# Queue order in the first feed-forward unit of an attention and Fourier-mixing kernel, and the steps at which v is loaded

## The chip, the core and the metric

The kernel runs on one core of a Trainium2 chip. The core has five engines, each with its own queue of instructions, which it takes in order: TensorE (PE: matmuls and transposes into PSUM), VectorE (DVE), ScalarE (ACT), GpSimd (POOL) and SyncE (SP), which here only issues DMAs. GpSimd issues DMAs too. Engines wait for each other, and for DMAs, through semaphores. A wait at the head of a queue holds back everything behind it on that engine.

The metric is the device time of one execution in microseconds (us). Three runs of the kernel before the change gave 2347.01, 2349.23 and 2350.73, so the median is 2349.23.

## What is computed

An attention block with talking heads feeds a Fourier mixing and a feed-forward block. The sizes are 8 batches, 12 heads, 448 rows, 64 columns for each head, so a model width of 768 and a feed-forward width of 3072. All is in float32.

```python
scores = scale * np.matmul(q, k.transpose(0, 1, 3, 2))
scores = np.einsum('bhij,hg->bgij', scores, w_pre)
scores = scores - np.max(scores, axis=-1, keepdims=True)
attn = np.exp(scores)
attn = attn / (np.sum(attn, axis=-1, keepdims=True) + 1e-09)
attn = np.einsum('bhij,hg->bgij', attn, w_post)
x = np.matmul(attn, v)           # then (B, H, S, D) -> (B, S, H*D)
...
X = np.fft.fft(np.fft.fft(x, axis=1), axis=2)
u = x + np.real(X)
un = (u - mean(u)) / np.sqrt(var(u) + 1e-06)
out = u + np.maximum(un @ w_ch1, 0.0) @ w_ch2
```

## The kernel before

**Attention part** (`mix_phase`). Each batch takes 23 steps, so there are 184 (`TOT`). Everything is put into lists with due times (`due(kind, at, fn)`) and emitted step by step. Within a step the operations follow a hand-written order that alternates between even and odd steps. In this part the order of emission is kept on PE, DVE, ACT and POOL, and a scheduler places SyncE's instructions. At each step the following happens:

- A gather brings rows of the scores from `Sb` into `Kr` (L605: four DMAs of 105 KB on SyncE, issued two steps before their use). TensorE mixes the heads on them (L616).
- ScalarE takes the exponential (L630), GpSimd scales by the reciprocal sums (L640), TensorE mixes again (L650), VectorE transposes (L663), and at some steps TensorE multiplies with v (L680).
- q, k and v of the next batch are loaded on GpSimd's DMA queue (L534, L543). v comes in three pairs of heads, each in two parts of 224 KB. The three buffers are single, so a part is loaded after the last use of its buffer by the batch before. `AT_V` holds the due steps: (3, 4), (5, 6) and (7, 7) of a batch.

When a batch has its attention rows `X`, GpSimd folds them for the Fourier transform. The steps of it are kept in the list `folds`: for each of two parities `pairs` twice (L745), `sides` (L750) and `quarters` (L759, L760); for the second pair of row groups come four times `both` (L766) at the end. The transform itself is two matmul stages (L789 and L805). VectorE adds the result to `X` (L816, L818), and the rows go to the scratch memory `u` or, reversed, `v` (L837 on SyncE; L828 and L834 on GpSimd). These stores wait in the list `later` and are emitted a step after their rows are done.

**Feed-forward part** (`ffn_phase`). The rows of all batches are cut into 7 tiles of 512. The hidden width is cut into 6 chunks. A unit is one chunk on one tile, `n = c * 7 + t`, and has two halves: `first` (hidden layer, L1169, with weights `w1t`) and `second` (output layer, L1247, with weights `w2t`). Both use a Strassen-like scheme with seven products.

The first unit overlaps with the end of the attention part: the last batch's Fourier steps are still to be done. What is left of them is a list `parts`, and `next_part()` puts one between two products. So in unit 0 these things happen on each queue:

- TensorE: the seven products of `first`, then the seven of `second`. Between the products of `second` stand the transposes of the next tile, `turn(1, x)` (L1108), for four groups of 128 rows, and some parts (L789, L805).
- VectorE: statistics of tile 1 (L1088, L1089), and adds from PSUM to the tile's rows (L1254).
- GpSimd: the foldings of the last batch (`fold_rest()`), and then `power(1)` (L375 to L378), which makes scale and bias from the statistics.
- ScalarE: `norm(1, x)` (L1099, scale and bias on 128 rows) and evictions of the transposes (L1110).
- SyncE: loads of the tiles' rows (`load_u`, L1067: twelve row pieces for a tile), loads of `w1t` and `w2t` (L1071, L1075: seven of 384 KB each), stores of tile 0's transposed rows to scratch (L1417: seven of 384 KB), stores of results (L1256) and of tile 1's transposed rows (L1119).

The chain to follow is stats, power, norm, turn. Transposes go to a PSUM buffer `psQ`; there are two of these, and the fourth product of `second` uses the same two.

Before the unit a small block keeps the emission order on PE, DVE and POOL for `lead.total` and `fold_rest`. The loop over units keeps it on PE and DVE alone; the scheduler places GpSimd's, SyncE's and ScalarE's instructions.

Of the kernel before, what the change touches and what calls it, by code (L numbers as in the profile page):

```python
# [60 lines left out]
TOT = B * GS  # L61
# [22 lines left out]
NTB = B * S // TB  # L84
# [3 lines left out]

AT_T = ((5, 9), (15, 17), (13, 15))
AT_L = ((-4, -3), (-2, -1), (0, 1), (2, 7), (11, 12), (13, 14))  # L90
AT_V = ((3, 4), (5, 6), (7, 7))
AT_QK = ((0, 2, 1), (0, 1, 2), (0, 1, 2), (1, 2, 2),
         (0, 1, 2), (0, 1, 2), (0, 1, 2), (0, 1, 2))
AT_AV = ((1, 2, 4), (0, 1, 3), (1, 3, 5), (1, 2, 4))
# [15 lines left out]
NC = 6  # L110
NM = DFF // 2 // P
NK = DM // 2 // P
FM = NM // NC
# [299 lines left out]
def mix_phase(ctx, tc, rest, ident, q, k, v, w_pre, w_post, u_scr, u_rev, wts, lead):  # L413
# [6 lines left out]
    nc = tc.nc  # L420
# [27 lines left out]
    pend, folds, later = [], [], []  # L448
# [60 lines left out]
    first = {}  # L509
# [333 lines left out]
    fill = {"QK": [], "AV": [], "full": [], "none": []}  # L843
# [7 lines left out]
    for b in range(B):  # L851
# [30 lines left out]
        for n in range(NG):  # L882
# [3 lines left out]
            at, gi = AT_X[n]  # L886
# [44 lines left out]
    ET = mybir.EngineType  # L931
    with tc.manual_schedule(engines={ET.PE, ET.DVE, ET.Activation, ET.Pool}):
        while s <= TOT - GS + AT_X[-1][0]:
            old = len(later)
            n = take("none", s)
# [30 lines left out]
        flush()  # L966
        wts.deal(1000)

    def fold_rest():
        while folds:  # L970
            folds.pop(0)()

    def part(fn, tile_fn):
        for _ in range(len(later)):
            later.pop(0)()
        while later and not fn:
            later.pop(0)()
        ms.append(tile_fn)
        if fn:
            for e in fn():  # L980
                e()

    assert not any(fill[k] for k in ("QK", "AV", "none"))
    return fold_rest, [lambda t, fn=fn: part(fn, t)
                       for _, _, fn in fill["full"] + [(0, 0, None)]]

# [7 lines left out]
ORDER = (0, 4, 5, 1, 6, 2, 3)  # L996
# [4 lines left out]
DEEP = 2  # L1001
# [6 lines left out]
def ffn_phase(ctx, tc, rest, ident, u_scr, u_rev, wts, ub_scr, out, fold_rest,  # L1008
# [4 lines left out]
    nc = tc.nc  # L1013

    def pool(name, bufs=1, **kw):
        return ctx.enter_context(
            tc.tile_pool(name=name, bufs=bufs, reuse_waits="tile", **kw))

    pub = pool("pub", 3)
# [4 lines left out]
    once = ExitStack()  # L1024
# [7 lines left out]
    pps = [pool("pps" + k, space=bass.MemoryType.PSUM) for k in "QPR"]  # L1032
    beside = ExitStack()
# [19 lines left out]
    us, ubs, w1, w2, wt = {}, {}, {}, {}, {}  # L1053
    right = {}
# [4 lines left out]
    def load_u(t):  # L1059
        if t % 3:  # L1060
            u = pu.tile([P, NT2, DM], F32, name="u", tag="u")
            us[t] = [u[:, x, :] for x in range(NT2)]
        else:
            us[t] = [lead.rows() for _ in range(NT2)]
        for x in range(NT2):
            for p0, m, src in _u_pieces(t, x, u_scr, u_rev):
                nc.sync.dma_start(out=us[t][x][p0:p0 + m, :], in_=src)  # L1067
# [5 lines left out]
    def load_w2(c, i):  # L1073
        w2[i] = pw2.tile([P, FM, DH], F32, name="w2t", tag=f"w2t{i}")
        nc.sync.dma_start(out=w2[i][:, :, :], in_=wts.w2[c][i])  # L1075
# [68 lines left out]
    def first(n, st, beside):  # L1144

        c, t = divmod(n, NTB)
        deep = c >= DEEP
        seed = n >= NTB + 2
        h = st["h"] = ph.tile([P, 7, FM, HT], F32, name="h", tag="h")
        if deep:  # L1150
            hq = st["hq"] = right["hq"].tile([P, 7, 4, P], F32, name="hq", tag="hq")
        h11, h22, h21, hs1, hs2, h12, h12s = (h[:, x] for x in range(7))
        norms = c == 0 and t + 1 < NTB
        vec = nc.vector
        ps = {}
        done = 0
        for k, i in enumerate(ORDER):
            if deep and t == 0:
                halves(ORDER2[k], (nc.vector, nc.gpsimd)[k % 2])
            if i in OPENS and ACC[i] not in ps:  # L1160
                ps[ACC[i]] = ps_tile(ACC[i])
            p = ps[ACC[i]].rearrange("p (m t) -> p m t", m=FM)
            ub = ubs.pop((n, i))
            for m in range(FM):
                for kc in range(NK):
                    for fn in beside.pop(done, ()):
                        fn()
                    done += 1
                    mm = nc.tensor.matmul(p[:, m, :], w1[i][:, kc, m * P:(m + 1) * P],  # L1169
                                          ub[:, kc, :],  # L1170
                                          start=i in (0, 4, 1)[:3 - seed] and m == kc == 0,
                                          stop=kc == NK - 1, skip_group_check=True)
                    if n == k == m == kc == 0:
                        tc.keep_in_program_order(mm)
            if i == 0 and seed:
                ps["Q"] = ps_tile("Q")
                nc.scalar.copy(out=ps["Q"][:, :], in_=ps["P"][:, :])
            elif i == 0:
                nc.scalar.copy(out=h11, in_=p)
            elif i == 4:  # L1180
                nc.scalar.copy(out=h22, in_=p)
            elif i == 5:
                nc.scalar.copy(out=h21, in_=p)
            elif i == 1 and seed:
                nc.scalar.activation(h11, p, ACTF.Relu)
            elif i == 1:
                vec.tensor_tensor(h11, h11, p, op=ALU.add)
                nc.scalar.activation(h11, h11, ACTF.Relu)
            elif i == 6:
                vec.tensor_tensor(h22, h22, p, op=ALU.add)  # L1190
                nc.scalar.activation(h22, h22, ACTF.Relu)  # L1191
                if deep:
                    quarters(nc.gpsimd, hq, h, H11, H22 + 1)
            elif i == 2:
                vec.tensor_tensor(h21, h21, p, op=ALU.add)
                nc.scalar.activation(h21, h21, ACTF.Relu)
            else:
                nc.scalar.activation(h12, p, ACTF.Relu)
            x = k - 2 * (n == 0)
            if norms and 0 <= x < NT2:  # L1200
                stats(t + 1, x)
                if x == NT2 - 1:
                    power(t + 1)
            if (n == 0 and k < 2) or (n == 1 and k not in (1, 2)):
                next_part()
                if n == 0 and k == 1:
                    fold_rest()
            if deep:
                wts.deal(DEALS[t > 0][k])
            elif i != 2:  # L1210
                wts.deal(2 if norms else 3 if c == 0 else 4)
            if i == 2:
                vec.tensor_tensor(hs1, h21, h22, op=ALU.add)
                vec.tensor_tensor(hs2, hs1, h11, op=ALU.subtract)
                if deep:
                    quarters(vec, hq, h, HS2, HS2 + 1)
                vec.tensor_tensor(h21, h11, h21, op=ALU.subtract)
            if t == NTB - 1 and c + 1 < NC:
                load_w1(c + 1, i)
            if NTB <= n + 1 < NC * NTB:  # L1220
                new_ub(n + 1, i)
                nc.sync.dma_start(out=ubs[n + 1, i][:, :, :],
                                  in_=ub_scr[(n + 1) % NTB][i])
        if deep:
            quarters(nc.gpsimd, hq, h, H12, H12 + 1)
            wts.deal(0)
        else:
            vec.tensor_tensor(h12s, h12, hs2, op=ALU.subtract)
        assert not beside
# [158 lines left out]

    for i in ORDER:
        load_w1(0, i)  # L1390
    load_u(1)
    us[0] = lead.u
    ET = mybir.EngineType
    with tc.manual_schedule(engines={ET.PE, ET.DVE, ET.Pool}):
        for n in range(1, 4):
            lead.total(n, pub)
        fold_rest()
    for i in ORDER:
        ubs[0, i] = lead.ub[i]
    with tc.manual_schedule(engines={ET.PE, ET.DVE}):  # L1400
        for i in ORDER:
            load_w2(0, i)
        parts_ = [(c, k) for c in range(1, NC) for k in range(NK + FM)]
        for n in range(DEEP * NTB):
            c, t = divmod(n, NTB)
            if c == 0 and 0 < t < NK + FM + 1:
                wts.add(*parts_.pop(0))
            while c and sum(o[1] for o in wts.ops) < 52:
                wts.add(*parts_.pop(0))
            wts.deal(0)  # L1410
            if n + 2 < NTB:
                load_u(n + 2)
            st = {}
            first(n, st, {})
            if n == 0:
                for i in ORDER:
                    nc.sync.dma_start(out=ub_scr[0][i], in_=lead.ub[i])  # L1417
            second(n, st)
            if c == 0:
                wts.deal(1000)  # L1420
            if n == 1:
                assert not parts
                rest.close()
                beside.close()
                pps.append(pool("ppy", space=bass.MemoryType.PSUM))
            if n == NTB - 1:
                once.close()
                for name, bufs in (("wt", 1), ("hq", 1), ("od", 9)):
                    right[name] = pool("p" + name, bufs, side="right")

    wts.eng = nc.sync
    SEAM = {49: 0, 50: 1, 51: 1, 52: 1, 53: 2, 54: 2, 55: 3, 56: 3, 57: 4, 58: 5, 59: 5}
    with tc.manual_schedule(engines={ET.PE, ET.DVE, ET.Activation, ET.Pool}):
        rest_ = {}
        for n in range(DEEP * NTB, NC * NTB):
            while parts_ and sum(o[1] for o in wts.ops) < 14:
                wts.add(*parts_.pop(0))
            st = {}
            at = second2(n, st)
# [79 lines left out]
```

## Time and profile before

| | us |
|---|---|
| median of three runs | 2349.23 |
| profiled execution | 2355.12 |
| its span | 2353.3 |
| TensorE busy | 2284.2 |
| VectorE busy | 1680.4 |
| GpSimd busy | 1141.5 |
| ScalarE busy | 1102.9 |
| first matmul L1169 of unit 0 starts | 827.9 |
| first matmul L1247 of unit 0 starts | 847.4 |
| first matmul L1169 of unit 1 starts | 881.6 |

The span runs from the first to the last instruction of one profiled execution, and the profiled execution's own time stands 1.8 us above it. Busy time is the time with at least one instruction under way. The mean granted clock of TensorE is 0.992 of full speed, so there are stretches in which the chip grants less.

Three kinds of views are used below. A list of waits says which engine and line waited for whom: us in total, times, longest. A chain of waits follows the work that ended last backwards, each step to what released it, and prints it in order of time. A table of windows gives, for each stretch of time, the busy time of each engine, the granted clock, the share of time for which the DMA engines were busy and what they moved.

### The profile page before, as it was taken

The page shows a single profiled execution, that of the slowest core. Times are in us where ns is not written, and L with a number is a line of the kernel's source. Part 1 is how long each engine was busy: PE and PEld are TensorE (multiplying, and loading weights), DVE is VectorE, ACT ScalarE, POOL GpSimd, SP SyncE. Part 2 cuts the span into 40 slices and gives each one's busy share as a digit, 9 for nine tenths or more (in the row PEclk, how much of TensorE's full clock was granted, in tenths as well). Part 3 has the DMA queues.
Part 4 walks back from the last instruction along what each step waited for, and adds up shares of the span by engine and source line. Part 5 has one row for each costly group of instructions (what it writes and reads, how often), then busy time and mean ns, then how long its engine had stood idle before and what let it go on. Part 6 is the DMA issues. An engine that isn't in the chain of part 4 may idle for free.

```text
span 2353.3 us, 59474 instructions
## 1 busy us (share of the span) xinstructions
PE 2284.2 (97%) x22600; PEld 1715.1 (73%) x22600; DVE 1680.4 (71%) x3596; ACT 1102.9 (47%) x3085; POOL 1141.5 (49%) x1692
## 2 busy tenths in 40 slices
PE   6999999999999989999999999999999999999998
PEld 3545555555555567777777779998999989999997
DVE  3768777787887747785676766678776777776556
ACT  4766766666676622322222233444444344444434
POOL 3577967878787542121343443335333533343333
PEclk8999999999999999999999999999999999999999
DMA  7565655656656566567887976549646945684553
GB/s 158 156 176 168 181 172 157 191 170 176 181 174 188 181 202 198 175 227 265 223 210 233 241 242 182 142 138 274 153 132 166 261 124 164 175 232 104 147 129 67
DMA packets 213481, 425.60 MB, mean 181 GB/s; under 512 B 39080, under 2 KB 135744, under 8 KB 213198
## 3 DMA queue, kind: packets, MB, share of 16 engines
q1 hardware_dynamic: 141758, 278.78, 34.8%
q0 software_dynamic: 65440, 141.05, 27.6%
q8 instruction: 181, 2.97, 0.5%
q10 hardware_dynamic: 6000, 1.97, 0.5%
q14 instruction: 102, 0.84, 0.1%
HBM read 213.16 MB, written 129.39 MB: 146 GB/s over the span
## 4 chain that ended last, share of the span: by engine, by line
PE 84%; DMA 4%; DVE 4%; ACT 3%; POOL 2%; issue 2%; SPq 1%; ACTq 0%; DVEq 0%; POOLq 0%
PE psP L1169 18%; PE psP L1304 10%; PE psR L1169 9%; PE mx L616 6%; PE psP L1247 6%; PE psR L1304 5%; PE ms L680 5%; PE ms L588 5%; PE psQ L1169 5%; PE po L650 4%; DMA Kr<-Sb 3%; PE psR L1247 3%; PE psQ L1304 3%; PE ms L805 2%; PE psQ L1247 1%
## 5 line engine op out<-in xcount | busy, mean ns | idle before, releaser
L640 POOL TENSOR_SCALAR PP<-PP,rcp 128x448 f32<-128x448 f32 x368 | 235.2, 649 | 210.7 <-DVE rcp L638 173.2
L630 ACT ACTIVATE PP<-mx,nmx 128x448 f32<-128x448 f32 x368 | 230.6, 631 | 191.0 <-DVE nmx L623 184.2
L623 DVE TENSOR_REDUCE nmx<-mx 128x1 f32<-128x448 f32 x368 | 213.4, 618 | 135.4 <-PE mx L616 133.3
L1338 POOL DMA_DIRECT2D out_dram<-od x109 | 133.2, 1408 | 280.9 <-DVE od L1335 158.0
L1133 POOL TENSOR_TENSOR hq<-h 128x256 f32<-128x256 f32 (+1 forms) x168 | 104.3, 621 | 292.2 <-ACT h L1191 171.7
L616 PE MATMUL mx<-Kr,kw 60*32 60x448 f32 x2944 | 216.5, 551 | 15.9 <-DMA Kr<-Sb 15.2
L1335 DVE TENSOR_TENSOR od<-od 128x768 f32<-128x768 f32 x196 | 189.0, 976 | 52.5 <-ACT od L1332 50.6
L588 PE MATMUL ms<-kT,qT 64*32 64x448 f32 (+1 forms) x3072 | 203.7, 550 | 8.4 <-ACT qT L451 6.6
L663 DVE STREAM_TRANSPOSE Pv<-po 128x896 f32<-128x896 f32 x184 | 203.6, 1107 | 7.2 <-PE po L650 5.0
L451 ACT COPY Sb<-ms 124x448 f32<-124x448 f32 (+1 forms) x384 | 184.5, 541 | 42.7 <-PE ms L588 27.7
L650 PE MATMUL po<-PP,kw 60*32 60x448 f32 x2944 | 197.0, 541 | 1.4 <-issue 1.4
L1332 ACT COPY od<-psP 128x192 f32<-128x192 f32 x390 | 125.0, 321 | 146.1 <-PE psP L1304 141.9
L680 PEld LDWEIGHTS ms<-Pv,vv 64*64 64x64 f32 x5376 | 137.8, 132 | 71.8 <-issue 54.1
L225 POOL DMA_DIRECT2D raw<-in_moe_w_ch_dram x88 | 52.4, 596 | 283.0 <-DVE tmp L269 267.3
L1169 PE MATMUL psP<-qs,w1t 128*128 128x256 f32 x744 | 177.3, 379 | 0.0
L1169 PE MATMUL psP<-ks,w1t 128*128 128x256 f32 x744 | 176.9, 379 | 0.1
L680 PE MATMUL ms<-Pv,vv 64*64 64x120 f32 (+1 forms) x5376 | 160.3, 263 | 1.5 <-ACT X L451 1.0
L1247 PE MATMUL psP<-w2t,h 128*128 128x384 f32 x448 | 153.8, 486 | 0.2 <-DVE od L1267 0.2
L1169 PEld LDWEIGHTS psP<-ks,w1t 128*128 128x128 f32 x744 | 139.8, 190 | 18.8 <-DVE u L1254 0.7
L1169 PEld LDWEIGHTS psP<-qs,w1t 128*128 128x128 f32 x744 | 139.8, 190 | 17.5 <-DMA w2t<-w 0.2
L1190 DVE TENSOR_TENSOR h<-h,psP 128x512 f32<-128x512 f32 x42 | 28.8, 686 | 142.6 <-PE psP L1169 142.3
L1169 PE MATMUL psP<-ub,w1t 128*128 128x256 f32 x528 | 126.4, 379 | 0.0
(194 smaller groups left out, 5124.5 us busy)
## 6 DMA issues: line engine op xcount, KB each, us to landing
Kr<-Sb SPq DMA_DIRECT2D x736, 105.0 KB
out_dram<-od POOLq DMA_DIRECT2D x137, 384.0 KB, 7.7
qs<-ub SPq DMA_DIRECT2D x89, 384.0 KB
ks<-ub SPq DMA_DIRECT2D x88, 384.0 KB
ub<-ub SPq DMA_DIRECT2D x79, 384.0 KB
w1t<-w SPq DMA_DIRECT2D x42, 384.0 KB
w2t<-w SPq DMA_DIRECT2D x42, 384.0 KB
raw<-in_moe_w_ch_dram POOLq DMA_DIRECT2D x56, 256.0 KB, 4.8
```

The lines of the kernel that those rows point to most:

```text
L588: nc.tensor.matmul(pss[x][o:o + hi - lo, :S], st["qT", xx][64 * x:64 * x + 64, y, lo:hi], st["kT", xx][64 * x:64 * x + 64, y, :], start=Tr ...
L616: nc.tensor.matmul(mx[x][64 * z + o:64 * z + o + 32, :S], kw1[64 * x:64 * x + KR, o:o + 32], Kr[64 * x:64 * x + KR, z, :], start=True, sto ...
L623: nc.vector.tensor_reduce(nmx[:, :], steps[T]["mx"][x][:, :S], axis=AX.X, op=ALU.max, negate=True)
L630: nc.scalar.activation(steps[T]["PP"][:, x, :], steps[T]["mx"][x][:, :S], ACTF.Exp, bias=steps[T]["nmx", x][:, :], accum_out=steps[T]["den ...
L640: nc.gpsimd.tensor_scalar(PP[:, x, :], PP[:, x, :], rcp[:, x:x + 1], 1.0, op0=ALU.mult, op1=ALU.mult)
L650: nc.tensor.matmul(po[o:o + 32, z, :S], kw2[64 * z:64 * z + KR, y, :], PP[64 * z:64 * z + KR, :, c * HS:(c + 1) * HS], start=True, stop=True)
L663: nc.vector.transpose(turned[a]["Pv"][:, j, :].rearrange("p (z s) -> p z s", z=2), steps[T]["po"][:, :, :S])
L680: nc.tensor.matmul(pss[y][64 * x:64 * x + 64, :nu * R], st["v", pr][64 * y:64 * y + 64, x, jb * D:(jb + 1) * D], _ap(Pv, 64 * y * rp + 32 ...
L1169: mm = nc.tensor.matmul(p[:, m, :], w1[i][:, kc, m * P:(m + 1) * P], ub[:, kc, :], start=i in (0, 4, 1)[:3 - seed] and m == kc == 0, stop= ...
L1247: nc.tensor.matmul(p, h[:, LHS[i], kf, x * P:(x + 1) * P], w2[i][:, kf, :], start=i in (0, 4, 1)[:3 - (c > 0)] and kf == 0, stop=kf == FM ...
L1304: nc.tensor.matmul(ps[j, key][:, :DQ], a, b, start=m in (0, 4), stop=True, skip_group_check=True)
L1335: eng.tensor_tensor(D[j][:, :, :], D[j][:, :, :], D[k][:, :, :], op=ALU.add)
```

## The change

The change has two parts.

First, `AT_V` becomes (2, 3), (4, 5), (6, 7): each of the six parts of v has a step of its own.

Second, in unit 0 the emission order is now kept on GpSimd and SyncE too. One context with PE, DVE, POOL and SP is opened before the unit and closed at its end; the loop goes on with PE and DVE. What is emitted first is therefore issued first on these two queues. The order of emission changes with it:

- `load_u(1)` is inside this context, and the `w2t` loads are emitted before the loop. Tile 2's loads (`load_u(2)`, in the loop ahead of `first`) come before the stores of tile 0's transposed rows, which are emitted between `first` and `second`.
- `fold_rest` takes a number. Where it took all foldings of the last batch after the second product of `first`, it now takes eight. The other four follow after the sixth product, behind `power(1)`, which is emitted just before.
- Parts that are due before step `TOT + 10` no longer empty the list `later` first.

```diff
-AT_V = ((3, 4), (5, 6), (7, 7))
+AT_V = ((2, 3), (4, 5), (6, 7))
...
-    def fold_rest():
-        while folds:
+    def fold_rest(n=1000):
+        for _ in range(min(n, len(folds))):
             folds.pop(0)()
 
-    def part(fn, tile_fn):
-        for _ in range(len(later)):
+    def part(fn, tile_fn, hold):
+        for _ in range(0 if hold else len(later)):
             later.pop(0)()
...
-    return fold_rest, [lambda t, fn=fn: part(fn, t)
-                       for _, _, fn in fill["full"] + [(0, 0, None)]]
+    return fold_rest, [lambda t, fn=fn, at=at: part(fn, t, at < TOT + 10)
+                       for at, _, fn in fill["full"] + [(TOT + 99, 0, None)]]
...
                 if n == 0 and k == 1:
-                    fold_rest()
+                    fold_rest(8)
+            if n == 0 and k == 5:
+                fold_rest()
...
-    load_u(1)
     us[0] = lead.u
     ET = mybir.EngineType
-    with tc.manual_schedule(engines={ET.PE, ET.DVE, ET.Pool}):
-        for n in range(1, 4):
-            lead.total(n, pub)
-        fold_rest()
+    order = ExitStack()
+    order.enter_context(tc.manual_schedule(engines={ET.PE, ET.DVE, ET.Pool, ET.SP}))
+    load_u(1)
+    for n in range(1, 4):
+        lead.total(n, pub)
     for i in ORDER:
         ubs[0, i] = lead.ub[i]
-    with tc.manual_schedule(engines={ET.PE, ET.DVE}):
-        for i in ORDER:
-            load_w2(0, i)
...
+        load_w2(0, i)
+    fold_rest()
...
+        if n == 0:
+            order.close()
+            order.enter_context(tc.manual_schedule(engines={ET.PE, ET.DVE}))
...
+    order.close()
```

ScalarE's instructions are placed by the scheduler in both kernels, and where one context ends and the next begins the scheduler may let instructions of the two pass each other. In the built program TensorE's order is unchanged. On VectorE three of tile 2's statistics and six operations on weights, which belong to unit 1, now stand inside unit 0, ahead of the adds from the fourth product of `second`. On ScalarE two evictions of transposes stand behind two norms that they preceded.

More of the change, by code (lines that the diff above doesn't have):

```diff
@@ L1390, in ffn_phase @@
         load_w1(0, i)
-    load_u(1)
     us[0] = lead.u
     ET = mybir.EngineType
-    with tc.manual_schedule(engines={ET.PE, ET.DVE, ET.Pool}):
-        for n in range(1, 4):
-            lead.total(n, pub)
-        fold_rest()
+    order = ExitStack()
[3 more added lines that the diff above has]
+        lead.total(n, pub)
     for i in ORDER:
         ubs[0, i] = lead.ub[i]
-    with tc.manual_schedule(engines={ET.PE, ET.DVE}):
-        for i in ORDER:
-            load_w2(0, i)
[L1403 to L1429, printed above, removed]
@@ new lines, in ffn_phase @@
+        load_w2(0, i)
+    fold_rest()
+    parts_ = [(c, k) for c in range(1, NC) for k in range(NK + FM)]
+    for n in range(DEEP * NTB):
+        c, t = divmod(n, NTB)
+        if c == 0 and 0 < t < NK + FM + 1:
+            wts.add(*parts_.pop(0))
+        while c and sum(o[1] for o in wts.ops) < 52:
+            wts.add(*parts_.pop(0))
+        wts.deal(0)
+        if n + 2 < NTB:
+            load_u(n + 2)
+        st = {}
+        first(n, st, {})
+        if n == 0:
+            for i in ORDER:
+                nc.sync.dma_start(out=ub_scr[0][i], in_=lead.ub[i])
+        second(n, st)
+        if c == 0:
+            wts.deal(1000)
+        if n == 0:
+            order.close()
+            order.enter_context(tc.manual_schedule(engines={ET.PE, ET.DVE}))
+        if n == 1:
+            assert not parts
+            rest.close()
+            beside.close()
+            pps.append(pool("ppy", space=bass.MemoryType.PSUM))
+        if n == NTB - 1:
+            once.close()
+            for name, bufs in (("wt", 1), ("hq", 1), ("od", 9)):
+                right[name] = pool("p" + name, bufs, side="right")
```

## The prediction

> **What bounds the kernel now.** I read the page's busy times first, then the waits of TensorE over the whole span, then the chain of waits and the timelines of the two places that the change touches.
>
> ```profile
> PE 2284.2 (97%) x22600; PEld 1715.1 (73%) x22600; DVE 1680.4 (71%) x3596; ACT 1102.9 (47%) x3085; POOL 1141.5 (49%) x1692
> ```
>
> TensorE is busy for 97%, so only what ends one of its waits, or gives it back clock, can shorten the run. Its waits, longest in total first (us in total, times, longest):
>
> ```profile
> PE mx L616 <- DMA Kr<-Sb: 15.2, 16, 2.9
> PE psP L1304 <- DVE od L1326: 11.4, 6, 2.7
> PE psQ L1108 <- ACT un L1099: 7.2, 1, 7.2
> ```
>
> The second lies in the last stages and is not touched. The third is one wait, in the first feed-forward unit; the first is spread over the attention part. The chain of waits around the third (start us, us, what):
>
> ```profile
> 846.31 0.96 POOL xf L766
> ...
> 848.22 0.96 POOL xf L766
> ...
> 851.84 2.28 POOL xf L766 x2
> ...
> 854.22 0.26 POOL mv L375
> ...
> 856.25 1.04 ACT un L1099
> ...
> 857.33 1.54 PE psQ L1108 x6
> ```
>
> TensorE ends its block of L1247 at 850.16 (timeline) and has nothing until the transposes of tile 1, at 857.33. They wait for norm (L1099), that for power (L375 to L378, GpSimd), and power stands in GpSimd's queue behind twelve folding steps, though the statistics it needs were complete at 846.9 (last L1089 of the tile). The same chain in the attention part, in batch 3:
>
> ```profile
> 363.80 8.30 DMA Kr<-Sb
> ...
> 372.15 1.76 PE mx L616 x9
> ```
>
> and the stretches of half a microsecond there (stretch and length; busy time of PE, PEld, DVE, ACT, POOL with counts; clock; DMA share; GB/s):
>
> ```profile
> 371.50:372.00 0.50, 0.00 (x0) 0.00 (x0) 0.00 (x0) 0.00 (x0) 0.50 (x2) 1.00 0.56 134
> 372.50:373.00 0.50, 0.50 (x10) 0.12 (x7) 0.00 (x0) 0.00 (x0) 0.50 (x1) 0.50 0.65 238
> ```
>
> A gather of 105 KB takes 8.3 us, TensorE idles 1.60 us, and then has half its clock from 372.05 to 375.45. Batch 5 repeats it: wait of 1.77 at 572.03, half clock from 573.4 to 576.8.
>
> **First feed-forward unit, GpSimd.** Only four of the twelve steps, the L766, move behind power. From the end of L745 at 846.31 there remain L750 (0.96), L759 x2 (1.16 in the row at 842.99, when VectorE left GpSimd alone; 2.0 beside it) and L760 (0.2): 848.7 instead of 854.2. Power took 2.0 us (854.22 to 856.23); the next tile's, beside a busy VectorE, 2.47 (894.98 to 897.45). Then L1099 with its start, 1.1. The transposes start between 851.8 and 852.3; I take 852.1. The wait shrinks from 7.17 to 1.9 us: **5.2 gained**. The four L766 end by 855.5; their reader L789 is at 867 or later.
>
> Before, the two windows after the stall ran at clock 0.5: six transposes took 1.54 us (0.82 at full clock, row at 861.99), the next L1247 block 3.48 (2.75). That is 1.45 us, gone if the clock holds: 6.7.
>
> **First unit, SyncE.** Its order becomes: two block stores of u (L837, the second waits for VectorE until 829.9 in both kernels), tile 1's twelve loads, w2t x7, tile 2's twelve loads, and only then the seven stores of tile 0's ub (L1417). Before, ub stores and w2t went out from 811 to 828, ahead of the loads. So w2t (7 x 384 KB, before 815 to 820) now comes after 835. First use 847.4, then one of 384 KB about every 3.5 us; in the 815 to 830 stretch such transfers moved at about 400 GB/s, one per microsecond. Hidden.
>
> The stores at the end are not free: the eviction of the first transposes (L1110, second half of the rows) reuses a buffer that the first ub store reads, and now waits for that store. Ahead of it on the queues from 829.9: 336 KB of u, 336 of v, tile loads 2 x 1536, raw weights 4 x 256, w2t 2688, itself 384. With 3.1 MB of it at 400 GB/s and 4.9 MB at the 272 GB/s that the row pieces got between 830 and 850, 26 us: 856. ScalarE reaches this eviction at about 858, since it now stands behind two later norms. Hidden by 2 us; every microsecond beyond 858 costs one. At 272 throughout it would be 859.4: 1.2 us lost.
>
> The same reordering costs something sure: with that PSUM buffer still full, the second tile's second group of transposes is put into the buffer of its first group and waits for its eviction (0.48 plus two handovers): **0.7 us**. From the transposes' start to the next L1247 block it is then 3.86 + 0.7 (before, 857.33 to 862.64 less the 1.45 of clock). That block starts at 856.7, ends at 859.4.
>
> **First unit, VectorE.** No edit aims at it, but in the built order three of tile 2's statistics (L1088, L1089) and six weight operations (L247 to L269) move ahead of the adds L1254 from psQ, that is from behind the unit's end. Before, they ran back to back here:
>
> ```profile
> 882.34 1.01 DVE L1088 BATCH_NORM_STATS2 st<-u 128x6 f32<-128x384 f32 x2
> ...
> 887.23 0.42 DVE L269 SCALAR_TENSOR_TENSOR tmp<-raw,tmp 128x256 f32<-128x256 uint32 x1
> ```
>
> 882.34 to 887.65: 5.3 us. They now start when VectorE has added the psP block, 0.58 after TensorE ends it, so the psQ adds end 6.4 and 6.9 after, the last transposes 7.4 after. Before it was 4.8 (865.39 to 870.16). **2.6 us lost**: a new wait PE psQ L1108 <- DVE of nearly 3 us. Where they came from, TensorE was not waiting for VectorE, so nothing comes back. Tile 2's loads are ahead of the ub store in the sum above, so there by 856.
>
> End of the last transposes: 859.4 + 7.4 = 866.8 against 870.16, **3.4 gained** before the clock.
>
> **The clock, rule and row.** [...] In stretches of 3.41 us laid on the edge at 372.05, the two were busy 56% and 48%; those busy 64% and more kept full clock, but so did feed-forward ones at 55% and 56%. The stretches of the new waits are some 20 to 60% busy; I take one halving: 3.4 - 1.7 = **1.7 us** for the unit. Bounds: 3.4 with none, 0 with two.
>
> **v one part a step.** L543 moves 224 KB each. Before, a batch loaded them in steps 3, 4, 5, 6, 7, 7; now one in each of 2 to 7. Step 7 loses one, step 2 gains one, 3 to 6 keep one. The DMA engines ran at a share of 0.85 to 0.93 after the pair at 362.9, at 240 GB/s: one load less brings the gather 0.95 us forward. The waits of 1.60 and 1.77 shrink to 0.7 and 0.8, their stretches rise above 75% busy and keep clock: 2 x (0.95 + 1.7) = 5.3. [...] A wait for vv itself (0.35 at 464.61) goes. At step 2 the buffer is free: the last matmul on it ends at 436.7 in batch 4, GpSimd comes to the load at 438.7. But the gathers in flight get 0.95 us more: batch 6 waits there already (0.96 at 647.76, after a gather of 8.35 us). I take 0.9 off; with a halving it is 2.6. Attention: 5.3 + 0.35 - 0.9 = **4.7 us**, bounds -5 and +6.
>
> **Sum.** 1.7 + 4.7 = 6.4 us off the profiled execution, 2355.1 (span 2353.3 and 1.8 around it): 2348.7. That execution is 5.9 us above the median, and waits for gathers are what may be fewer in the others; I count 0.7 of the attention part, 3.3, the unit's in full: 2349.2 - 5.0 = **2344.2**, own range 2341.5 to 2346.5.
>
> **Rivals.**
> 1. *No change.* Gathers are late only in some executions, or step 2 gives back what step 7 gains; the unit's 1.7 us alone: 2347.5. For it: waits at step 7 in two of seven batches only, and the 5.9 us. Against: both cost clock, the same way.
> 2. *More.* No halving in the unit, no price at step 2: 3.4 + 5.6 = 9.0, 2340.2. For it: feed-forward stretches at 55% that kept full clock. Against: the 2.9 us wait.
> 3. *Slower.* The load in step 2, beside the load of q there, delays the gathers that steps 4 and 5 use, and each batch pays 0.95 + 1.7 = 2.65. It decides from five batches: 13.3 - 7.4 = 5.9 lost, 2355. For it: waits of 0.42 and 1.24 at 153 to 156, and that at 647.76. Against: step 2 holds 868 KB with gathers (420) and q (224); step 7 in batch 3 held 1.7 MB with its weights.
>
> **Numbers.** About 0.2% (4.7 us) can be told from no change. The forecast has 0.46 (0.28 below 2344.5, the rest within), rival 1 0.22, rival 2 0.18, rival 3 0.14. Faster 0.46, same 0.40, slower 0.14. The range, 2338.5 to 2352.5, takes in rivals 1 and 2 and part of 3.
>
> **What would show it.** Right: PE psQ L1108 <- ACT un near 2 us; a new wait of psQ L1108 for DVE near 3; L1110 not waiting for DMA; no wait of L616 above 1 us nine microseconds after a batch's last v load. Wrong: L1110 or L1088 waiting for a DMA of ub or u; L1247 waiting for w2t; new waits for Kr five steps into a batch; no halved stretch, or two, in the unit.

## The result and the profile after

The changed kernel is faster. 22 executions of each kernel, on the same chip and in turns, gave a median of 2340.45 us (2335.0 to 2352.22) against 2351.11 (2345.55 to 2356.43) before. The ratio is 0.9958, with a 95% interval of 0.9947 to 0.997, so some 9.9 us are gone (7 to 12.5). Two later comparisons of the same kernel gave 0.9948 (0.9933 to 0.9962) and 0.9958 (0.9942 to 0.9975). The profiled execution took 2343.49 us, with a span of 2341.7.

TensorE stays at 97%, from the busy times of the page:

```profile
PE 2281.3 (97%) x22600; PEld 1717.1 (73%) x22600; DVE 1677.4 (72%) x3596; ACT 1101.0 (47%) x3085; POOL 1140.6 (49%) x1692
```

Its waits over the whole span (us in total, times, longest), in the changed kernel:

```profile
PE psP L1306 <- DVE od L1328: 11.4, 6, 2.7
PE mx L616 <- DMA Kr<-Sb: 11.1, 9, 2.9
...
PE psQ L1108 <- ACT un L1099: 3.3, 1, 3.3
PE psQ L1108 <- DVE ur L1256: 2.9, 2, 2.6
```

The wait for the gathered rows has gone from 15.2 to 11.1 us, and from 16 times to 9. The one for the normalised rows `un` has gone from 7.2 to 3.3. The first row is the old wait of the last stages, two lines further down in the file. The last row has grown; before, at the old line numbers, it was

```profile
PE psQ L1108 <- DVE ur L1254: 0.6, 2, 0.3
```

This is GpSimd's way to the transposes of tile 1 (timeline of the changed kernel: start us, us, engine and instruction, and in brackets the idle time before it with what released it):

```profile
831.12 1.00 POOL L750 TENSOR_TENSOR xs<-xs 113x383 f32<-113x383 f32 x1
...
833.27 0.65 POOL L760 COPY xq<-xs 113x1 f32<-113x1 f32 x1
...
834.01 0.69 POOL L375 TENSOR_SCALAR mv<-mv 128x4 f32<-128x4 f32 x1
...
834.79 1.34 POOL L376 TENSOR_TENSOR mv<-mv,mhalf 128x4 f32<-128x4 f32 x1
...
836.71 2.92 POOL L766 TENSOR_TENSOR xf<-xq 113x385 f32<-113x385 f32 x3
836.77 1.95 ACT L1099 ACTIVATE un<-u,mv 128x768 f32<-128x768 f32 x2 [3.66 <-POOL mv L378]
...
837.85 0.88 PE L1108 MATMUL psQ<-ident,un 128*128 128x128 f32 x6 [3.32 <-ACT un L1099]
```

The four L766 stand behind power as planned (this view ends with the third of them). Power itself runs from 834.01 to 836.74, so 2.7 us, while VectorE is busy without a gap.

And this is VectorE, eleven microseconds later in the same timeline:

```profile
848.76 0.24 DVE L247 TENSOR_SCALAR tmp<-raw 128x256 uint32<-128x256 uint32 x1
...
849.25 1.01 DVE L1088 BATCH_NORM_STATS2 st<-u 128x6 f32<-128x384 f32 x2
...
852.49 0.43 DVE L269 SCALAR_TENSOR_TENSOR tmp<-raw,tmp 128x256 f32<-128x256 uint32 x1
852.83 1.01 DVE L1256 TENSOR_TENSOR ur<-ur,psQ 128x384 f32<-128x384 f32 x2
...
853.43 0.47 PE L1108 MATMUL psQ<-ident,un 128*128 128x128 f32 x1 [2.60 <-DVE ur L1256]
```

The adds from `psQ` stand behind tile 2's statistics and the weight operations, and TensorE's last transposes wait 2.6 us for them.

In the attention part, the place in batch 3 that was shown before, nine to ten steps into the batch (stretch and length; busy time of PE, PEld, DVE, ACT, POOL with counts; clock; DMA share; GB/s), in the changed kernel:

```profile
366.00:370.00 4.00, 4.00 (x54) 2.02 (x52) 3.79 (x8) 2.71 (x8) 3.92 (x7) 1.00 0.44 158
370.00:374.00 4.00, 4.00 (x114) 2.57 (x116) 2.52 (x8) 2.27 (x9) 3.84 (x6) 1.00 0.37 139
```

TensorE is busy throughout, at full clock, and the DMA engines are busy for 0.37 to 0.44. In batch 5 something is left. The chain of waits there (start us, us, what):

```profile
555.15 8.56 DMA Kr<-Sb
...
563.76 0.94 PE mx L616 x8
```

The gather still takes 8.6 us and is still late, by 0.9 us, but the granted clock stays at 1.00 there.

### The profile page after: what moved, and what is told of

It reads as the page before. It is cut to its first block, busy times and chain, and to the rows that moved or that the text cites. A ratio compares the mean times of both kernels' runs of the same rounds, so it can differ in the third digit from the quotient of the medians.

```text
span 2341.7 us, 59482 instructions
## 1 busy us (share of the span) xinstructions
PE 2281.3 (97%) x22600; PEld 1717.1 (73%) x22600; DVE 1677.4 (72%) x3596; ACT 1101.0 (47%) x3085; POOL 1140.6 (49%) x1692
## 4 chain that ended last, share of the span: by engine, by line
PE 87%; DMA 4%; DVE 4%; ACT 2%; issue 1%; POOL 1%; SPq 1%; ACTq 0%; DVEq 0%; POOLq 0%
PE psP L1169 18%; PE psP L1306 10%; PE psR L1169 9%; PE mx L616 6%; PE psP L1249 6%; PE ms L680 6%; PE ms L588 5%; PE psR L1306 5%; PE psQ L1169 5%; PE po L650 5%; PE psR L1249 3%; DMA Kr<-Sb 3%; PE psQ L1306 3%; PE ms L805 2%; PE psQ L1249 1%; PE ms L562 1%
## 5 line engine op out<-in xcount | busy, mean ns | idle before, releaser
L616 PE MATMUL mx<-Kr,kw 60*32 60x448 f32 x2944 | 212.5, 549 | 11.6 <-DMA Kr<-Sb 11.1
L663 DVE STREAM_TRANSPOSE Pv<-po 128x896 f32<-128x896 f32 x184 | 203.8, 1108 | 4.3 <-PE po L650 2.1
L1169 PE MATMUL psP<-qs,w1t 128*128 128x256 f32 x744 | 177.3, 379 | 0.0
L1169 PE MATMUL psP<-ks,w1t 128*128 128x256 f32 x744 | 176.8, 379 | 0.1
L1169 PEld LDWEIGHTS psP<-ks,w1t 128*128 128x128 f32 x744 | 139.9, 190 | 18.5 <-DVE u L1256 0.7
L1169 PEld LDWEIGHTS psP<-qs,w1t 128*128 128x128 f32 x744 | 139.8, 190 | 17.5 <-issue 0.2
L1169 PE MATMUL psP<-ub,w1t 128*128 128x256 f32 x528 | 126.4, 379 | 0.0
```

Source lines behind the costliest of these rows:

```text
L616: nc.tensor.matmul(mx[x][64 * z + o:64 * z + o + 32, :S], kw1[64 * x:64 * x + KR, o:o + 32], Kr[64 * x:64 * x + KR, z, :], start=True, sto ...
L663: nc.vector.transpose(turned[a]["Pv"][:, j, :].rearrange("p (z s) -> p z s", z=2), steps[T]["po"][:, :, :S])
```

## A first reading that fell

Read as a pair, the two profiles say something different from the prediction. The first unit begins at 812.2 us instead of 827.9, so what lies ahead of the unit is 15.6 us shorter. The unit, from its first L1169 to that of unit 1, takes 56.4 us instead of 53.7. The theory that went into the first experiments was therefore: *v brings everything, in all seven later batches, and the edit of the unit costs 2.7 us.* The rival was the prediction's own split, a few microseconds from each.

## Experiments

Each run gave a timed comparison with the kernel before (6 to 12 executions on its side) and one profile. Four measures are taken from every profile. *Attention* is the time from the first step of batch 1 to the last step of batch 7 (starts of L663). *Halved* is the number of 3.4 us stretches in it at half clock. *Waits* is the sum of TensorE's waits in it. *Tail* is the time from the last step to the first L1169 of unit 1; the two columns behind it are TensorE's waits in the tail, for `un` and for the adds from `psQ`. Times are in us.

| run | v due at steps | ratio (95% interval) | attention | halved | waits | tail | `un` | adds |
|---|---|---|---|---|---|---|---|---|
| before | 3 4 5 6 7 7 | 1 | 680.5 | 2 | 15.6 | 65.9 | 7.2 | 0.3 |
| e2_queue_only | 3 4 5 6 7 7 | 0.9987 (0.9968-1.0005) | 678.0 | 1 | 13.9 | 65.8 | 2.4 | 2.6 |
| e8_hold_order_old_v | 3 4 5 6 7 7 | 0.9984 (0.9968-0.9999) | 670.4 | 0 | 11.7 | 60.8 | 1.8 | 0.3 |
| changed | 2 3 4 5 6 7 | 0.9958 (0.9947-0.997) | 667.6 | 0 | 10.7 | 67.4 | 3.3 | 2.6 |
| e5_changed_again | 2 3 4 5 6 7 | 0.9948 (0.9933-0.9962) | 668.9 | 0 | 11.4 | 64.6 | 3.4 | 2.6 |
| e12_changed_third | 2 3 4 5 6 7 | 0.9958 (0.9942-0.9975) | 668.7 | 0 | 11.0 | 62.7 | 2.4 | 2.6 |
| e1_v_only | 2 3 4 5 6 7 | 0.9975 (0.996-0.9991) | 672.2 | 0 | 12.8 | 66.6 | 6.9 | 0.3 |
| e3_nest | 2 3 4 5 6 7 | 0.9952 (0.9937-0.9966) | 674.9 | 0 | 11.4 | 60.0 | 1.8 | 0.3 |
| e9_hold_order_again | 2 3 4 5 6 7 | 0.9962 (0.9949-0.9975) | 668.5 | 0 | 8.3 | 63.5 | 1.8 | 0.3 |
| e6_hold_order_no_sync | 2 3 4 5 6 7 | 0.9948 (0.9929-0.9966) | 667.3 | 0 | 9.1 | 62.6 | 0.5 | 0.3 |
| e10_six_foldings | 2 3 4 5 6 7 | 0.9961 (0.9946-0.9975) | 667.7 | 0 | 8.6 | 63.0 | - | 0.3 |
| e11_one_load_in_step_7 | 2 3 4 5 6 8 | 0.9963 (0.9946-0.9979) | 667.8 | 0 | 9.0 | 61.9 | 2.4 | 0.3 |
| e4_v_last8 | 3 4 5 6 7 8 | 0.9991 (0.9978-1.0003) | 671.9 | 1 | 10.0 | 66.3 | 6.5 | 0.3 |
| e7_three_more_in_step_7 | 3 4 7 7 7 7 | 1.0069 (1.0044-1.0094) | 692.3 | 9 | 28.9 | 67.2 | 6.6 | 0.3 |

### e1_v_only and e2_queue_only: one half of the change each

```diff
-AT_V = ((3, 4), (5, 6), (7, 7))
+AT_V = ((2, 3), (4, 5), (6, 7))
```

This is e1, on the kernel before. e2 is the reverse edit on the changed kernel.

> The kernel before with the new table of the v loads alone. Theory (the attention gains in all seven later batches, the feed-forward edit costs 2.7 us): the whole gain of the change and those 2.7 us on top, 12 to 13 us below the kernel before, a ratio near 0.9948; L616's waits for gathered K rows fall as in the changed kernel. Rival (the sum of the prediction, attention 4.7 us and the rest from the feed-forward unit): 4.7 us below, a ratio near 0.998.

> The changed kernel with the old table of the v loads, so that only the first feed-forward unit differs from the kernel before. Theory: the unit loses some 2.7 us, a ratio of 1.001, with the wait of the second transposes for psQ at the adds near 2.9 us and three windows of half clock in the unit. Rival (the prediction's unit): a gain of 1.7 to 5 us, a ratio of 0.998 to 0.9993.

Measured: v alone 0.9975, some 6 us (2 to 9.4); the unit's edit alone 0.9987, some 3 us (a gain of 7.5 to a loss of 1.2). The theory's 0.9948 lies outside the interval of e1, and so does its 1.001 for e2; its loss of 2.7 us in the unit has no support: e2's tail is 65.8 against 65.9 before. The rival's 0.998 for e1 holds, and its 0.998 to 0.9993 for e2. The two halves add up to 9 us, about the whole gain. That e2 gains anything is not shown by itself, since its interval holds 1. For v two other pairs of ratios agree with e1: the changed kernel against e2 (0.9958 and 0.9987), and e3 and e9 against e8 (0.9952 and 0.9962, 0.9984), which is 5 to 7.5 us. So the 15.6 us were in part the scatter of one execution against another. The table shows how wide that is: with the old order of v the attention took 680.5, 678.0 and 670.4 us in three executions, with the new one 667.3 to 674.9 in eight. A piece of it can be named: batch 7 took 86.9 us in the profile before and 87.3 in e3's, with the new table, but 83.2 to 85.0 in the other twelve, so these 3 us are not v's.

### e3_nest: VectorE's order held over the end of the unit

```diff
-    order = ExitStack()
-    order.enter_context(tc.manual_schedule(engines={ET.PE, ET.DVE, ET.Pool, ET.SP}))
+    order, whole = ExitStack(), ExitStack(); whole.enter_context(tc.manual_schedule(engines={ET.PE, ET.DVE}))
+    order.enter_context(tc.manual_schedule(engines={ET.Pool, ET.SP}))
...
             order.close()
-            order.enter_context(tc.manual_schedule(engines={ET.PE, ET.DVE}))
...
-    order.close()
+    whole.close()
```

The nine instructions of unit 1 then stay behind the adds. TensorE, GpSimd and SyncE keep the order of the changed kernel.

> The changed kernel, but the order of TensorE and VectorE is held over the end of the first unit, so that the third tile's three statistics and the six weight operations stay behind the adds they were put ahead of; GpSimd and sync as in the changed kernel. Theory (that chain is the new wait of 2.6 us and brings a half-clock window after it): 3 to 5 us below the changed kernel, a ratio near 0.994, the wait psQ L1108 for DVE L1256 gone and the window of half clock behind it too. Rival (the three statistics are then late for the next tile and the same time is lost in unit 1): within 1 us of the changed kernel, a ratio near 0.996.

The wait for the adds is back at 0.3 us. In the list of waits of e3 this is left of the two:

```profile
PE psQ L1108 <- ACT un L1099: 1.8, 1, 1.8
...
PE psQ L1108 <- DVE ur L1256: 0.6, 2, 0.3
```

The tail has no halved stretch and takes 60.0 us. e8 repeats that (60.8); e9, the same kernel as e3, has one halved stretch and takes 63.5. The four tails of the changed order take 62.7 to 67.4. From unit 1 to the end the three hold runs took 1472.0, 1475.6 and 1472.5 us, the changed order 1471.9 to 1473.1, so no clear loss shows there, though e8's 1475.6 is 2.5 us above the next of these. In the tail the theory holds for the wait, and in two of three profiles for the clock. The time does not show it: the interval of e3 holds the theory's 0.994 and the changed kernel's 0.9958 alike.

### e4_v_last8 and e11_one_load_in_step_7: what step 7's loads cost

```diff
-AT_V = ((3, 4), (5, 6), (7, 7))
+AT_V = ((3, 4), (5, 6), (7, 8))
```

This is e4, on the kernel before. e11 has (2, 3), (4, 5), (6, 8), on the kernel of e3.

> The kernel before with one number changed: the last v load goes from step 7, where it was the third load, to step 8, nothing is put into step 2. Theory (what cost time was that step 7 issued three loads ahead of its gathers): as good as the whole new table or better, 11 to 14 us below the kernel before, a ratio of 0.994 to 0.9955. Rival (all v loads coming one step earlier is what helps, or the last one is needed early): no gain, a ratio of 0.999 to 1.002.

> As e9_hold_order_again, with the last v load in step 8 in place of step 7, so that step 7 has one load (k or q) only. Theory (each load fewer ahead of step 7's gathers is worth what the first one was, 0.9 us a batch): steps 0 of batch 1 to the end of the attention 3 to 6 us shorter than with the new table (667 to 675 us there). Rival (with two loads the gathers are off the edge, and a load in step 8 pushes step 8's): the same within 2 us or longer.

e4: 0.9991, with an interval from 0.9978 to 1.0003. The theory's 0.994 to 0.9955 lies outside, and the rival's no gain inside (0.999 to 1.002). The profile's attention (671.9) is as short as with the whole new table, yet it holds a halved stretch, in batch 4. Whether taking a load out of step 7 is enough, or all loads must come earlier, is not settled by it. e11: attention 667.8, inside the range of the new table (667.3 to 674.9); the rival holds, one load fewer in step 7 brings no more time. The waits of L616 at the two places, eight to nine steps into batches 3 and 5, do follow the number of loads in step 7. With three loads (before, e2, e8) they are 1.0 to 1.6 us in batch 3 and 1.8 to 2.8 in batch 5. With two they are 0 to 0.3 and 0.8 to 2.1 with the new table, and 0.2 and 1.3 in e4. With one, in e11, there is none. So the delay by step 7's loads is shown at these places; that removing it alone shortens the run is not. In e11 TensorE waits for v instead, 0.9 us in step 9 of batch 4.

### e7_three_more_in_step_7: five loads in the step

```diff
-AT_V = ((3, 4), (5, 6), (7, 7))
+AT_V = ((3, 4), (7, 7), (7, 7))
```

The step has two loads more than before, not three as the run's name says: four of v and one of q or k.

> The kernel before with the last four v loads all in step 7 (five loads there in place of three, steps 4 to 6 with one or none). Theory (what costs is the number of loads that stand ahead of step 7's gathers, 1 to 2 us for each more in the batches where the gather is on the edge): 7 to 20 us above the kernel before, a ratio of 1.003 to 1.0085, and waits of L616 for gathered rows nine to eleven steps into nearly every batch. Rival (only the number of loads of a batch and the queue's total time matter): within 2 us, a ratio of 0.999 to 1.001.

The size is as expected (1.0069, 16 us), the mechanism is not. TensorE's longest waits in e7:

```profile
PE ms L680 <- DMA vv<-in_v_dram: 20.9, 12, 5.1
...
PE mx L616 <- DMA Kr<-Sb: 9.5, 8, 2.9
```

It waits for v itself, in step 8 of batches 1 to 6, by 0.9 to 6.0 us; the wait for gathers is smaller than before (9.5 us, 15.2 before). Here the crowded loads are late for their own reader, and nine halved stretches follow. What five loads cost the gathers can't be read from this run, since TensorE stops for v first.

### e5, e8, e6: a second profile, and the parts of the unit

```diff
-    order.enter_context(tc.manual_schedule(engines={ET.Pool, ET.SP}))
+    order.enter_context(tc.manual_schedule(engines={ET.Pool}))
```

This is e6, on the kernel of e3. e8 is the kernel of e3 with the old `AT_V`; e5 is the changed kernel.

> The changed kernel once more, for a second profiled execution and for a comparison on the same chip as the next three. If what the v loads bring is as large as the two first profiles show (the first unit began 15.6 us earlier), the unit begins before 815 us again; if that was mostly the scatter of single executions, it begins between 815 and 825. The unit itself takes 54 to 57 us in either case, and the ratio is 0.994 to 0.998.

> As the run that holds the order of VectorE over the end of the unit, but sync's own order is left to the scheduler, so that the block stores and the third tile's loads stand where the kernel before had them; GpSimd's order stays written out. Theory (of the unit's gain GpSimd's order is nearly all, sync's hides nothing and costs nothing): the unit takes 48 to 49.5 us as there, a ratio of 0.994 to 0.9965. Rival (the late stores of the blocks are needed, the evictions of the second tile wait for them): the unit is 2 us or more longer than there.

> The run that holds VectorE's order over the end of the unit, with the old table of the v loads: the feed-forward edit alone, without the statistics put ahead of the adds. Theory (the unit falls from 53.8 to 48 or 49 us, and 0.5 to 1.5 us of it come back later): 3.5 to 5.5 us below the kernel before, a ratio of 0.9977 to 0.9985, and the unit begins at 815 us or later. Rival (what is won in the unit is lost in the units behind it): a ratio of 0.9995 to 1.0005.

e5's unit begins at 813.6 us and takes 53.6, just under the 54 to 57 expected. By its expectation the early begin speaks for the large effect of v, but e9, e3 and e6 have the same order of v and begin at 817.0, 823.9 and 820.5, so the split of e1 and e2 stands. e8: 0.9984, 3.8 us, in the theory's range, but its interval reaches 0.9999, into the rival's. The unit took 49.7 us (48 or 49 expected) and began at 817.0 (815 or later expected). What lies behind it was some 3 us longer than on average in the other profiles, where 0.5 to 1.5 were expected.

e6 (0.9948) shows what SyncE's order does. Its unit is the shortest of all (47.2 us, where the theory said 48 to 49.5; `un` is awaited for 0.5), so the rival falls. But the theory's *hides nothing* falls too: the way from the last step to the unit takes 15.4 us, against 11.1 to 11.8 in e3, e8 and e9. ScalarE's eviction of the attention rows, in the last microseconds ahead of the unit, in e6:

```profile
811.10 0.86 ACT L451 COPY X<-ms 113x384 f32<-113x384 f32 x2 [4.09 <-DMA u<-X]
```

and in the changed kernel:

```profile
804.49 0.86 ACT L451 COPY X<-ms 113x384 f32<-113x384 f32 x2 [1.31 <-PE ms L724]
```

In e6 it waits for the store of `X` to `u` (L837), and TensorE for it (2.7 us), with a halved stretch behind. SyncE issues that store behind two of the block stores (L1417), as in the kernel before. In all nine profiles with SyncE in emission order that store goes first and TensorE releases the eviction; in all five without, the DMA does.

### e9, e10, e12: power earlier still

```diff
-                    fold_rest(8)
+                    fold_rest(6)
```

This is e10, on the kernel of e3. e9 repeats e3 and e12 the changed kernel, on the same chip.

> The run that holds VectorE's order over the end of the unit once more, on one chip with the changed kernel. The stretch from the last step of the attention to the start of the second unit takes 60 to 61 us (64.6 to 67.4 in the changed kernel); if these 5 us are not lost elsewhere, the median is 3 to 7 us below the changed kernel's, a ratio to the kernel before of 0.992 to 0.995.

> As e9_hold_order_again, with the power on GpSimd behind six foldings in place of eight (four instructions, 4.3 us, of GpSimd go behind it). Theory (GpSimd's place alone sets when the transposes of the second tile start): the wait of psQ L1108 for un goes from 1.8 us to nothing, the stretch is 1.8 us shorter, 58 to 59.5 us. Rival (behind it ScalarE's own queue or VectorE's statistics end at the same time): the stretch stays at 60 to 61 us and L1108 waits for something else.

> The changed kernel a third time, as the other side of the comparison with e9_hold_order_again: a ratio of 0.994 to 0.997, 64 to 68 us from the last step to the second unit.

In e10 the wait for `un` is gone and another has its place. Its list of waits:

```profile
PE psQ L1108 <- ACT qs L1110: 4.3, 2, 3.7
```

and ScalarE's timeline:

```profile
846.00 0.99 ACT L1110 COPY qs<-psQ 128x384 f32<-128x384 f32 x2 [4.64 <-DMA ub<-qs]
```

The eviction waits for the late store of tile 0's block. With the changed order (changed, e2, e5, e12) that wait is 0.4 us in one profile of four and absent in the others; in e3, e8 and e9 it is 1.1, 2.6 and 2.9, and in e10 4.6. The sooner the transposes came in these runs, the more of the store's delay was seen. The tail is 63.0, with one halved stretch, where the theory said 58 to 59.5 and the rival 60 to 61. The rival holds in that L1108 waits for something else; that this is a store's DMA was in neither.

e9 and e12 have medians of 2342.41 and 2342.64; 3 to 7 us between them were expected. Both tails lie outside what was expected, 63.5 for 60 to 61 and 62.7 for 64 to 68. The tails differ by 3.7 us on average (61.4 in the hold runs, 65.1 in the changed order), and a difference of that size is within what two such intervals leave open. No version here is shown to beat the changed kernel.

## Why the prediction was right, and where it was off

The forecast was a gain of 5.0 us on the median, and about 10 came. The measured 2340.45 lies in the full range, but under the prediction's own range of 2341.5 to 2346.5. The direction and the waits that it named were right; the term of the attention was mis-sized. Rival 2 names almost the measured time (2340.2), but not for its reasons: the unit has halved stretches, and step 2 has its price.

**v.** The prediction found 4.7 us and counted 3.3. Over the profiles the mean attention is 676.3 us with the old table (three) and 669.5 with the new (eight), so 6.8; e1 gives 6 (2 to 9.4). Of the 6.8, the waits and halved stretches explain 5.0: each profile's waits plus 1.7 us for each halved stretch come to 15.4 on average with the old table and 10.4 with the new. The rest lies in no listed wait and stays open; the 3 us of batch 7 make some of it.

The places were right. The wait eight to nine steps into batch 3 was 1.6, 1.0 and 1.2 us with the old table, and 0 to 0.3 with the new; in batch 5 it was 1.8 to 2.8 and became 0.8 to 2.1. There were three halved stretches in three executions, and none in eight. With 1.7 us for each, the two places bring 3.8 us on average, where 5.3 were forecast.

Two steps fell short. The discount, *waits for gathers are what may be fewer in the others*, 0.7 of the term, is right for the two places (two halved stretches, one, none), but the whole term came out larger than 4.7 and not smaller (by time alone 3.3 can't be excluded, since the interval of e1 holds it). And the rest of the attention, set at a loss of 0.5, brought a gain of 3.

The price at step 2 is real: waits of L616 two steps into batch 5, 0.8 us on average with the new table (0 to 1.4) against 0.2. The prediction put 0.9 into batch 6. Rival 3 needed it in five batches.

**The unit's sum.** It forecast 1.7 us. The mean tail is 66.5 us for the old order (before, e1, e4, e7) and 65.1 for the changed (changed, e2, e5, e12): 1.4. Term by term, on the same means:

| | forecast | measured |
|---|---|---|
| wait for `un` | 5.2 gained | 3.9 gained (6.8 to 2.9) |
| second transposes behind the first's eviction | 0.7 lost | 0.6 lost |
| adds behind tile 2's statistics | 2.6 lost | 2.3 lost (0.3 to 2.6, in all four profiles) |
| half clock while TensorE works | 1.45 gained, 1.7 lost | 2.2 before, 2.4 after: 0.2 lost |
| eviction of `X` ahead of the unit | not seen | 1.0 gained (last step to the unit: 12.4 to 11.4) |

The terms come to a gain of 1.8; the other 0.4 were not traced. In the changed kernel's profile power took 2.7 us beside VectorE instead of 2.0 to 2.5, and the foldings between the last L745 and power took 3.0 instead of 2.4. With both the wait is 3.3 us there, and 2.9 on average, instead of 1.9. The gain ahead of the unit was missed although SyncE's order was written down: the first L837 was named, but not the engine that had waited for it while it stood behind two stores of tile 0's blocks, ScalarE with its eviction of `X`.

**The store behind the loads.** "Hidden by 2 us" was right for the changed kernel, as the wait of 0.4 at most shows, and so was its warning: e3, e8, e9 and e10 bring the transposes sooner and run into it.

**The clock.** The traces follow the prediction's measure, how busy TensorE is in a whole stretch. The two stretches that it gives as 56% and 48% busy are those with the waits of 1.60 us in batch 3 and 1.77 us in batch 5. The half clock behind them lasted 3.4 us each time (372.05 to 375.45 in batch 3); the 1.7 us that the prediction counts for one halving are half of that. All changes of the clock in a trace lie on a grid of 3.41 us, to 2 ns. These are the stretches of that grid around the wait in the changed kernel (stretch and length; busy time of PE, PEld, DVE, ACT, POOL with counts; clock; DMA share; GB/s):

```profile
849.46:852.87 3.41, 1.37 (x5) 0.48 (x3) 3.27 (x11) 0.00 (x0) 0.00 (x0) 1.00 0.27 104
852.87:856.29 3.42, 2.86 (x15) 2.86 (x15) 1.93 (x4) 0.96 (x2) 0.66 (x1) 0.50 0.54 151
856.29:859.70 3.41, 3.41 (x7) 1.90 (x7) 0.56 (x1) 0.53 (x1) 0.00 (x0) 0.50 0.11 41
```

and in the same kernel's second profile (e5), with the same wait of 2.6 us:

```profile
853.31:856.72 3.41, 1.87 (x15) 1.68 (x16) 2.66 (x7) 0.98 (x3) 0.66 (x1) 1.00 0.33 73
856.72:860.13 3.41, 3.41 (x17) 2.29 (x16) 1.60 (x4) 0.57 (x2) 0.00 (x0) 1.00 0.47 177
```

In the first execution most of the wait falls into one stretch, TensorE is busy for 40% of it, and two stretches at half clock follow. (The second of them comes after one that was busy for 84% at half clock.) In the second execution the wait is shared between two stretches, the emptier one is busy for 55%, and none follows. e2 (39%, one) and e12 (54%, none) agree. So the outcome goes with where the wait falls on the grid, and that differs from one execution to the next. In the four profiles of the changed order the whole tail has three, two, one and no halved stretches, and takes 67.4, 65.8, 64.6 and 62.7 us in that order. "One halving" was near the mean of one and a half; the bounds of none and two were one too narrow.

## What to carry to other kernels

Where single executions of one kernel differ by 10 us (2345.55 to 2356.43 before), a pair of profiles can't divide a gain of 10 us among its causes: run each half alone, and take lengths of the same stretch over all profiles. A queue's new order has to be followed for every buffer that its DMAs release, in front of the place it was made for too. In the changed kernel SyncE issued its two L837 at 800.42 and 814.27 us and the first tile load behind them at 814.68; in the kernel before they went out at 814.87 and 829.89, with all seven `w2t` loads between them. And where an order written by hand ends, look at what another engine pulls over that edge: here it took back 2.3 of the 3.9 us that the edit had won in its unit.

## What was not expected of the hardware

Half clock after a short wait goes with where the wait falls, and not with its length alone. The same wait of 2.6 us for the adds was followed by 6.8 us at half clock in one execution and by none in two others of the same program (e5, e12). Over all 14 profiles, from 100 us on, the stretches of the 3.41 us grid at full clock sort by TensorE's busy share alone. All 39 that were busy for 41% or less were followed by half clock. None of the 9062 busy for more than 56% was. Of the 43 in between nine were, so what decides there is not known. At half clock the full clock came back after every stretch busy for 87% or more and after none at 79% or less. By the author's estimate, half of its 3.41 us, a halved stretch costs 1.7 us where TensorE is busy. The tails of the changed order (given above) rise by 1.2 to 1.9 us with each.
